# Eight unread loads of 1 to 8 partitions ahead of the first K tile of a cached-attention decode kernel

## The chip, the cores and the metric

The kernel runs on one core of one Trainium2 chip. The core has a matrix engine (TensorE, PE in the profile, with PEld for its weight loads), a vector engine (VectorE, DVE), a scalar engine (ScalarE, ACT), GpSimd (POOL) and SyncE (SP), which here does nothing but issue loads. Loads and stores are carried out by 16 DMA engines between HBM and the on-chip memory SBUF, which has 128 partitions. Time is the device time of one execution in microseconds, the median of the runs. A profiled execution gives the trace from which the views below are taken; its span is a little shorter than the time of the run.

## What is computed

One decode step for one token x of 448 numbers: grouped-query attention over a cache of 65536 positions (16 query heads, 8 key/value heads of 256), a gated feed-forward layer, and a sigmoid gate g that mixes the two.

```python
q = (x @ wq) -> 16 heads of 256
scores = q . k_cache * 256 ** -0.5        # each k/v head serves 2 query heads
a = (softmax(scores) . v_cache) @ wo
gate, up = x @ W_gate, x @ W_up
b = ((gate * (gate > 0)) * up) @ W_down
out = g * a + (1 - g) * b                 # g = sigmoid(sum(x * gate_w))
```

Everything is bfloat16. K and V caches are 8 x 65536 x 256 each, 537 MB together; the weights wq, wo, W_gate, W_up and W_down add some 12 MB. So nearly all of the work is to bring the caches in once.

## The kernel before

**Tiles and slots.** A tile is 128 partitions x 128 positions x 256, 64 KB in each partition, 8 MB in all; a head has four K tiles and four V tiles, which makes 32 and 32. Three ring buffers of that size (`ring[0..2]`, line 135) hold them. `order` (lines 206 to 220) writes the sequence of the loads by hand: wq, gate and up, K tile 0, W_down, K tiles 1, 2 and 3, and from then on one V tile (of the head before) after each K tile from tile 3 on. Near the end come pieces of wo and the last V tile in four pieces. Slots are given out in turn (line 236), and `freed` keeps for each load what must be finished before its slot is overwritten.

**Planner.** Each operation is given to an engine with a key, a planned time; `finish` sorts the operations of each engine by key, and that is the order of its program. Loads go to SyncE. `emit` puts a wait ahead of an operation for what it depends on. A load's semaphore counts 16 when it has landed. Loads of one queue are therefore issued in the order of their keys, and a load that waits for its slot holds up those behind it.

**The first loads.** The keys are 3.0 for the first 384 rows of wq (line 470, into `ring[2]`), 3.001 and 3.002 for gate and up (line 487), 3.01 for the tail of wq (line 471, into the first 2048 columns of `ring[1]`), 3.012 for the tail of gate (line 489). K tile 0 (line 535, into `ring[0]`) follows, then the tail of W_up in eight loads of four partitions (`rows64`, line 380), then W_down (line 522, into `ring[2]` once the q matmuls are done), then K tile 1 into `ring[1]`. `held` (line 230) names the first users of the slots: `ring[1]` is free for K tile 1 after `q`, the last q matmuls (line 327); `ring[2]` is free for K tile 2 after `gu` and `dn`, the feed-forward matmuls (lines 498 to 527).

**A K tile's way.** When it has landed, VectorE transposes it in two halves (line 353), TensorE forms the scores (lines 368 and 394; many matmuls of several functions are recorded under 394), VectorE and ScalarE take the maximum and the exponential (lines 541 to 545). The scores of a K tile free its slot. After the fourth K tile of a head its weights are rescaled and transposed (lines 551 to 571). A V tile needs only the matmuls of lines 441 and 394. The end is the wo matmuls (line 618), the copy out (line 623) and the store (line 625).

**Feed-forward.** Gate and up are multiplied early (line 498), their tails when they land (lines 506 and 510); VectorE applies gate and product (lines 516 to 520) between the two transposes of K tile 0, and TensorE the down projection (line 527).

Of the kernel before, what the change touches and what calls it, by code (L numbers as in the profile page):

```python
# [24 lines left out]
class _Plan:  # L25
# [13 lines left out]
    def dma(self, eng, key, sem, fn, deps=()):  # L39
        if sem not in self.dsem:  # L40
            self.dsem[sem] = self.es.enter_context(self.nc.semaphore("d_" + sem))
        o = _Op(eng, key, fn, deps, dma=sem)
        self.ops.append(o)
        return o
# [46 lines left out]
def bass_gated_mix__gqa_block_cached__glu_gated_reglu__decode_kernel(  # L91
# [39 lines left out]
    with es:  # L131
# [3 lines left out]
        ring = [sb("ring%d" % i, [128, U * DH], BF) for i in range(NRING)]  # L135
# [60 lines left out]
        op, dma = pl.op, pl.dma  # L196
# [30 lines left out]
        T_END = t + 20.0  # L227


        slot, held, freed = {}, {1: ["q"], 2: ["gu", "dn"]}, {}  # L230
        r = 0
        for kind, i, _ in order:
            if kind in ("k", "v") or (kind, i) in (("wo", 0), ("vp", 0)):
# [150 lines left out]
        l_, qk, smax, aexp, pv, last = {}, {}, {}, {}, {}, {}  # L384
# [83 lines left out]
        for kind, i, t in issue:  # L468
            if kind == "wq":
                l_["wq"] = dma("sp", t, "wq", lambda e: e.dma_start(wq3, A_wq[0:NR3, :].rearrange("(p k) n -> p (k n)", k=R3)))  # L470
                l_["wqh"] = dma("sp", t + 0.01, "wqh", lambda e: e.dma_start(
                    wqa, A_wq[NR3:D, :].rearrange("r (c n) -> (r c) n", c=2)))
                tq = tL["wq", 0]
# [57 lines left out]
            elif kind == "k":  # L531
                n = i
# [44 lines left out]
            elif kind in ("v", "vp"):  # L577
                if kind == "v":
                    n, lo, hi = i, 0, U
# [84 lines left out]
```

## Time and profile before

| | us |
|---|---|
| time, median of 2 runs | 1279.15 (1278.81 to 1279.49) |
| time of the profiled execution | 1278.8 |
| its span | 1277.3 |
| mean granted TensorE clock | 0.628 of full speed |

The busy times of the page are sums over the span. Its section on DMA counts packets: one packet is one contiguous piece that a DMA engine moved. In the list of issues a row names destination and source, the queue that issued (SPq is SyncE's), the number of loads of that kind, KB of each, and the median time from issue to landing in us. In the order in time, a row has start and duration in us, engine, line, operation, destination and source, a count, and in brackets the idle time of the engine before it and what ended it. In the table of stretches, a row has the stretch in us, its length, the busy time and instruction count of PE, PEld, DVE, ACT and POOL, then the granted clock, the busy share of the DMA engines and GB/s. A row of the waits has who waited for whom, the total in us, how often, and the longest.

### The profile page before, as it was taken

Reading aid. Unit: us, or ns where it says so; the run is one execution under the profiler, and the core shown is the slowest. Engines: PE = TensorE matmul, PEld = TensorE weight load, DVE = VectorE, ACT = ScalarE, POOL = GpSimd, SP = SyncE. Lnnn points to the kernel's source line nnn. Section 1 sums busy time; section 2 is a strip of 40 time slices with the busy share of each in tenths; the row PEclk is TensorE's granted clock in tenths of the full one; section 3 lists DMA queues with packets and bytes.
Section 4 is the critical chain, followed back from the end, with each engine's and each line's share of the span. In section 5 each row is a group of like instructions: output and inputs, shape, how many; then the busy total and the mean of one; then the engine's idle time right before and its main releaser. Section 6 shows DMA issues by size and latency. Waiting matters only on the chain.

```text
span 1277.3 us, 6839 instructions
## 1 busy us (share of the span) xinstructions
PE 353.3 (28%) x4410; PEld 71.3 (6%) x1862; DVE 688.2 (54%) x310; ACT 51.3 (4%) x84; POOL 7.3 (1%) x21
## 2 busy tenths in 40 slices
PE   3223223313122241133220242211332213223135
PEld 2000000000000000000000000000000000000001
DVE  3698743575534655445555554556535666336511
ACT  0000000000000000000000000000000000000000
POOL 2000000000000000000000000000000000000000
PEclk9566666665666575666755666656666556666576
DMA  9999999999999999999999999999999999999998
GB/s 405 442 426 431 438 437 432 427 433 438 435 429 427 439 434 433 434 429 433 432 435 436 431 432 429 436 441 429 427 434 437 436 429 427 438 439 432 427 428 352
DMA packets 11906, 549.46 MB, mean 430 GB/s; under 512 B 1315, under 2 KB 1574, under 8 KB 2790
## 3 DMA queue, kind: packets, MB, share of 16 engines
q1 hardware_dynamic: 11874, 549.03, 99.6%
q8 instruction: 24, 0.39, 0.1%
q14 instruction: 4, 0.03, 0.0%
q10 hardware_dynamic: 4, 0.00, 0.0%
HBM read 549.03 MB, written 0.00 MB: 430 GB/s over the span
## 4 chain that ended last, share of the span: by engine, by line
DVE 38%; DMA 31%; PE 17%; another core or an unknown queue 12%; issue 1%; SPq 0%; ACT 0%
DVE ring L353 31%; DMA ring<-in_A_k_cache_dram 28%; PE ST L368 5%; PE ST L394 5%; PE O L394 4%; DMA ring<-in_A_wo_dram 3%; DVE o_sb L403 2%; PE O L441 1%; DVE P L564 1%; DVE P L562 1%; DVE ST L541 1%; DVE nmb L543 1%; PE M_ps L569 0%; PE M_ps L557 0%
## 5 line engine op out<-in xcount | busy, mean ns | idle before, releaser
L353 DVE STREAM_TRANSPOSE ring<-ring 128x8192 uint32<-128x8192 uint32 x64 | 554.2, 8692 | 315.0 <-DMA ring<-in_A_k_cache_dram 315.0
L368 PE MATMUL ST<-ring,xm 128*16 128x512 bf16 x1024 | 141.6, 544 | 770.2 <-DVE ring L353 770.2
L394 PE MATMUL ST<-ring,xm 128*16 128x512 bf16 x1024 | 138.5, 532 | 0.0
L394 PE MATMUL O<-ring,P 128*32 128x512 bf16 x1512 | 117.2, 421 | 0.0
L541 DVE COPY_PREDICATED ST<-bm,ST 128x512 f32<-128x512 uint16 x32 | 22.2, 693 | 170.7 <-PE ST L394 170.7
L545 ACT ACTIVATE P<-ST,nmb 128x512 bf16<-128x512 f32 x32 | 45.4, 1417 | 1142.8 <-DVE nmb L543 1142.8
L368 PEld LDWEIGHTS ST<-ring,xm 128*16 128x16 bf16 x1024 | 32.2, 116 | 928.4 <-DVE ring L353 798.2
L441 PE MATMUL O<-ring,P 128*32 128x512 bf16 (+1 forms) x536 | 58.7, 438 | 27.3 <-DMA ring<-in_A_v_cache_dram 27.3
L403 DVE CAST_PREDICATED o_sb<-bm,O 128x512 bf16<-128x512 uint16 (+1 forms) x33 | 22.3, 679 | 62.6 <-PE O L394 56.4
L562 DVE TENSOR_TENSOR P<-P,hs 128x2048 bf16<-128x2048 bf16 x8 | 18.3, 2292 | 8.6 <-ACT hs L559 8.6
L441 PEld LDWEIGHTS O<-ring,P 128*32 128x32 bf16 (+1 forms) x536 | 16.0, 113 | 123.8 <-issue 91.5
L543 DVE TENSOR_REDUCE nmb<-ST 128x1 f32<-128x512 f32 x32 | 22.1, 691 | 1.1
L564 DVE STREAM_TRANSPOSE P<-P 128x2048 bf16<-128x2048 bf16 x8 | 18.5, 2311 | 0.3
L569 PE MATMUL M_ps<-hs,ones_f 128*128 128x2 f32 x16 | 4.7, 363 | 46.0 <-DVE hs L568 46.0
L421 PE MATMUL M_ps<-emat,o_sb 128*128 128x2 bf16 x72 | 3.3, 168 | 22.4 <-DVE o_sb L413 22.4
L545 ACT ACTIVATION_READ_ACCUMULATOR P<-ST,nmb 128x1 f32 x32 | 8.6, 268 | 0.0
L320 PE MATMUL M_ps<-ring,P 128*128 128x256 bf16 x48 | 7.6, 335 | 1.7 <-DMA ring<-in_A_wq_dram 1.7
L569 PEld LDWEIGHTS M_ps<-hs,ones_f 128*128 128x128 f32 x16 | 4.0, 311 | 46.7 <-DVE hs L568 46.7
L555 PE MATMUL M_ps<-identf,hs 128*2 128x128 f32 x8 | 2.2, 278 | 15.8 <-DVE hs L553 15.8
L320 PEld LDWEIGHTS M_ps<-ring,P 128*128 128x128 bf16 x48 | 5.6, 119 | 3.5 <-DMA ring<-in_A_wq_dram 1.8
L461 DVE TENSOR_SCALAR attnT<-M_ps,hs 64x4 bf16<-64x4 f32 x16 | 3.5, 221 | 3.8 <-PE M_ps L421 3.7
L618 PE MATMUL A_ps<-ring,attnT 128*1 128x224 bf16 x64 | 5.4, 320 | 0.2
(86 smaller groups left out, 70.5 us busy)
## 6 DMA issues: line engine op xcount, KB each, us to landing
ring<-in_A_v_cache_dram SPq DMA_DIRECT2D x1, 4096.0 KB, 29.8
ring<-in_A_wq_dram SPq DMA_DIRECT2D x1, 3072.0 KB, 10.3
ring<-in_A_v_cache_dram SPq DMA_DIRECT2D x1, 2048.0 KB, 34.3
ring<-in_A_v_cache_dram SPq DMA_DIRECT2D x2, 1024.0 KB, 37.3
ring<-in_A_wo_dram SPq DMA_DIRECT2D x4, 448.0 KB, 39.2
ring<-in_B_W_down_dram SPq DMA_DIRECT2D x1, 1568.0 KB, 23.4
ring<-in_B_W_gate_dram SPq DMA_DIRECT2D x1, 1344.0 KB, 13.0
ring<-in_B_W_up_dram SPq DMA_DIRECT2D x1, 1344.0 KB, 15.8
```

The lines of the kernel that those rows point to most:

```text
L320: ins = e.matmul(QN_ps, xw3[:, kt, 31 - j:159 - j], wq3[:, kt * NQ + j * 256:kt * NQ + (j + 1) * 256], start=(j == 0 and kt == 0), stop=Fa ...
L353: return lambda e: e.transpose(v, v)
L368: ins = e.matmul(o, xm[:, x0:x0 + 16], v, start=st, stop=False, skip_group_check=True, tile_position=(0, 32 * w))
L394: return e.add_instruction(mybir.InstMatmult(name=nc.get_next_instruction_name(), engine=e.engine, ins=[e.lower_ap(v), e.lower_ap(w, for_m ...
L403: return e.copy_predicated(dst, m.to_broadcast(list(src.shape)), src)
L441: ins = e.matmul(o, w, v, start=st, stop=False, skip_group_check=True, tile_position=(0, 32 * g))
L541: join = op("dv", tk + 25.2, lambda e: e.copy_predicated(ST[0][:], bm[:, NB:NB + 1].bitcast(mybir.dt.uint16).to_broadcast([128, 512]), ST[ ...
L543: smax[n] = op("dv", tk + 26, lambda e, n=n, NM=NM, t_=t_: e.tensor_reduce(NM[:, t_:t_ + 1], ST[0][:], AX.X, ALU.max, negate=True), [join, ...
L545: aexp[n] = op("ac", tk + 27, lambda e, n=n, t_=t_, NM=NM, RS=RS, Ph=Ph: e.activation(Ph[:, t_:2048:4], ST[0][:], ACTF.Exp, bias=NM[:, t_: ...
L562: rsc = op("dv", T + 16, lambda e, X=X, pb=pb: e.tensor_tensor(pb, pb, X[:, 12:16].unsqueeze(1).to_broadcast([128, 512, 4]), ALU.mult), [h ...
L564: last["ev", h] = [op("dv", T + 17, lambda e, Ph=Ph: e.transpose(Ph[:], Ph[:]), [rsc])]
L569: l3 = mop("pe", T + 19, lambda e, X=X: e.matmul(LS_ps, ones_f[:, :], X[:, 6:8], start=True, stop=True), [l2, c_one])
```

## The change

Eight loads are added to SyncE's queue. Load i, for i from 0 to 7, brings the first 3 x (i + 1) rows of wq, three rows of 8 KB for each partition, into i + 1 partitions of `ring[1]`: partition i // 2 and every eighth one after it, 24 KB in each, at column 8192 for even i and 20480 for odd i. No two loads write the same place, none touches the wq tail in the first 2048 columns, and nothing reads them. They share one semaphore, and K tile 1, which overwrites `ring[1]`, waits for it. Their keys, 3.02 to 3.027, put them after the tail of gate and before K tile 0. The result of the kernel does not depend on them.

```diff
-        slot, held, freed = {}, {1: ["q"], 2: ["gu", "dn"]}, {}
+        slot, held, freed = {}, {1: ["q", "pk"], 2: ["gu", "dn"]}, {}
...
             if kind == "wq":
                 l_["wq"] = dma("sp", t, "wq", lambda e: e.dma_start(wq3, A_wq[0:NR3, :].rearrange("(p k) n -> p (k n)", k=R3)))
+                for i in range(8):
+                    c = 8192 + i % 2 * 12288
+                    l_["pk"] = dma("sp", 3.02 + 0.001 * i, "pk", lambda e, i=i, c=c: e.dma_start(
+                        ring[1][i // 2:i // 2 + 8 * i + 1:8, c:c + 12288], A_wq[0:3 * i + 3, :].rearrange("(p k) n -> p (k n)", k=3)))
                 l_["wqh"] = dma("sp", t + 0.01, "wqh", lambda e: e.dma_start(
                     wqa, A_wq[NR3:D, :].rearrange("r (c n) -> (r c) n", c=2)))
```

## The prediction

> **What bounds the kernel now.** I read the busy times and slices of the page first, then the stretches, then the issues of the DMA queue, then the order in time of SyncE and of VectorE's big transposes.
>
> ```profile
> span 1277.3 us, 6839 instructions
> ...
> PE 353.3 (28%) x4410; PEld 71.3 (6%) x1862; DVE 688.2 (54%) x310; ACT 51.3 (4%) x84; POOL 7.3 (1%) x21
> ...
> DMA  9999999999999999999999999999999999999998
> ...
> DMA packets 11906, 549.46 MB, mean 430 GB/s; under 512 B 1315, under 2 KB 1574, under 8 KB 2790
> ...
> q1 hardware_dynamic: 11874, 549.03, 99.6%
> q8 instruction: 24, 0.39, 0.1%
> ...
> DVE 38%; DMA 31%; PE 17%; another core or an unknown queue 12%; issue 1%; SPq 0%; ACT 0%
> ```
>
> No compute engine is busy for more than 54% of the span, while SyncE's queue (q1) keeps the 16 DMA engines at work for 99.6% of it. The chain of waits gives DVE 38%, which misleads if read alone: it follows one tile's latency back, not the resource that is full. The stretches show at what rate that full resource runs:
>
> ```profile
> 0.00:20.00 20.00, 9.61 (x68) 7.44 (x69) 7.95 (x29) 1.49 (x2) 7.26 (x21) 1.00 0.94 385
> ...
> 80.00:1180.00 1100.00, 297.14 (x3795) 52.23 (x1491) 611.47 (x236) 45.82 (x74) 0.00 (x0) 0.62 1.00 433
> 1180.00:1200.00 20.00, 0.37 (x8) 0.29 (x8) 12.00 (x5) 0.00 (x0) 0.00 (x0) 0.50 1.03 446
> ...
> 1220.00:1225.00 5.00, 4.68 (x54) 1.00 (x18) 0.95 (x4) 0.00 (x0) 0.00 (x0) 0.62 0.78 330
> ```
>
> The last two columns are DMA share and GB/s: 433 GB/s at a share of 1.00 through the steady part, that is 433 / 16 = 27.06 GB/s for one engine. So the time is bytes over rate, and what counts is the bytes of the engine that has most of them: a tile has landed only when its last engine has brought its rows.
>
> **The queue must stay full for this to hold.** The issues, with the time from issue to landing:
>
> ```profile
> ring<-in_A_wq_dram SPq DMA_DIRECT2D x1, 3072.0 KB, 10.3
> ...
> ring<-in_B_W_down_dram SPq DMA_DIRECT2D x1, 1568.0 KB, 23.4
> ring<-in_B_W_gate_dram SPq DMA_DIRECT2D x1, 1344.0 KB, 13.0
> ring<-in_B_W_up_dram SPq DMA_DIRECT2D x1, 1344.0 KB, 15.8
> ...
> ring<-in_A_wq_dram SPq DMA_DIRECT2D x1, 512.0 KB, 16.6
> ring<-in_A_k_cache_dram SPq DMA_DIRECT2D x32, 50.4
> ring<-in_A_v_cache_dram SPq DMA_DIRECT2D x31, 34.8
> ...
> ring<-in_B_W_gate_dram SPq DMA_DIRECT2D x1, 224.0 KB, 16.6
> ring<-in_B_W_up_dram SPq DMA_DIRECT2D x8, 28.0 KB
> ```
>
> and the landings of K tiles, read from the start of the transpose that waited for each:
>
> ```profile
> 38.71 8.71 DVE L353 STREAM_TRANSPOSE ring<-ring 128x8192 uint32<-128x8192 uint32 x1 [15.19 <-DMA ring<-in_A_k_cache_dram]
> ...
> 63.55 8.71 DVE L353 STREAM_TRANSPOSE ring<-ring 128x8192 uint32<-128x8192 uint32 x1 [4.17 <-DMA ring<-in_A_k_cache_dram]
> ...
> 102.78 8.71 DVE L353 STREAM_TRANSPOSE ring<-ring 128x8192 uint32<-128x8192 uint32 x1 [0.70 <-DMA ring<-in_A_k_cache_dram]
> ...
> 141.48 17.30 DVE L353 STREAM_TRANSPOSE ring<-ring 128x8192 uint32<-128x8192 uint32 x2 [4.99 <-DMA ring<-in_A_k_cache_dram]
> ...
> 1188.48 17.30 DVE L353 STREAM_TRANSPOSE ring<-ring 128x8192 uint32<-128x8192 uint32 x2 [7.52 <-DMA ring<-in_A_k_cache_dram]
> ```
>
> From K tile 3 on a V tile lies between two K tiles, so 141.48 - 102.78 = 38.70 us is two tiles: 19.35 us each. A V tile lands 34.8 us after its issue, so 34.8 - 19.35 = 15.4 us of older work is still ahead of it. That is the reserve against a dry queue.
>
> **What a load of few rows does to the engines.** The added loads have 1 to 8 rows, so the first question is on how many engines such a load runs. Counted in the code, 80 loads have 128 rows (32 K, 31 V, 4 V pieces, 2 wq, 2 gate, 1 up, 1 down, 7 wo), the eight 28 KB loads of W_up have 4 partitions, and x, gate_w and out have one. If each load leaves one tiny packet on each engine that it uses, 80 x 16 + 8 x 4 + 3 = 1315, which is the page's count under 512 B to the unit. With the 4-row loads on 16 engines it would be 1411. So a 4-row load runs on 4 engines. Are they the same four each time? Between the landings of K tiles 0 and 1 lie 63.55 - 38.71 = 24.84 us; one tile is 19.35, W_down (1.606 MB at 433 GB/s) 3.71, which leaves 1.78 us for the eight 28 KB loads. On the same four engines they cost 229,376 B / (4 x 27.06 GB/s) = 2.12 us, spread over all 16 only 0.53. The 1.78 is near the 2.12 (the engine last with tile 0 need not be one of the four). Small loads pile up on the same engines. The same 1.78 us speaks for no fixed cost by the load. [...]
>
> **The bytes, step by step.** Load i (0 to 7) has i + 1 rows of 24 KB, together 36 rows, 864 KB. If they pile up as W_up's do, each load starting at the same engine, that engine gets 8 rows, the next 7, and so on to the eighth with 1; the other eight get none. One row: 24,576 B / 27.06 GB/s = 0.908 us. First engine: 8 x 0.908 = 7.3 us. Since that engine never runs dry and all K and V tiles give it the same eighth-of-128 share as the others, the delay stays with it to the end, and the last landing moves by as much.
>
> Two corrections. The price of a row may be higher at the start of the program: the wq load has the same packets, eight rows of 24 KB on each engine, and took 10.3 us from issue to landing, first latency and receipt included. So the eight rows cost 7.3 to 10.3. And part may be hidden: from K tile 3 to K tile 31 are 28 x 2 = 56 tiles, 1083.6 us at 19.35, but 1188.48 - 102.78 = 1085.70, so the latest engine has fallen back by 2.1 us during the run (the 24 instruction packets on q8 are the likely cause, 0.1% of 16 x 1277.3 us). If those are other engines than the first, 2.1 us of lateness exist already and the added lateness goes beside them. So 5.2 to 10.3 in all. The corrections have opposite signs and about the same size, so I take the plain row at steady rate, 7.3.
>
> **Issue and waits.** SyncE's start:
>
> ```profile
> 2.75 0.51 SPq L489 DMA_DIRECT2D ring<-in_B_W_gate_dram  x1
> 3.30 0.45 SPq L535 DMA_DIRECT2D ring<-in_A_k_cache_dram  x1
> 3.82 5.47 SPq L380 DMA_DIRECT2D ring<-in_B_W_up_dram  x8
> 20.80 0.35 SPq L522 DMA_DIRECT2D ring<-in_B_W_down_dram  x1
> 21.19 44.11 SPq L535 DMA_DIRECT2D ring<-in_A_k_cache_dram  x3
> ```
>
> Eight more issues at 0.45 (the K row) to 0.68 us (5.47 / 8) are 3.6 to 5.5 us of SyncE. K tile 0 then goes out at 6.9 to 8.8 instead of 3.30. Ahead of it on the engines lie 3072 + 1344 + 1344 + 512 + 224 = 6496 KB, 6.65 MB, at 385 GB/s 17.3 us of work, so the issue costs nothing; it would cost its excess if it came after 17. The W_up pieces go out by 14.8 instead of 9.3, still before W_down, which waits until 20.80 for the q matmuls (wq and its tail are ahead of the new loads and do not move). K tile 1 gains a wait: its slot now also needs the new loads landed, at 17.3 + 7.3 = 24.6 to 28 us by queue order, instead of issue at 21.19. Queued behind it on SyncE are K tiles 2 and 3. Tile 0 lands only at 38.71, so the cover is 10 us or more: price zero. K tile 2 is the longest one to look at:
>
> ```profile
> SPq L535 <- PE A_ps L527: 32.0, 1, 32.0
> ```
>
> It waits 32.0 us for the down projection, which follows tile 0's first transpose on VectorE and so moves with tile 0's landing, 21.5 + 32.0 = 53.5 to about 60.8. On the late engine tile 1 then ends at 63.55 + 7.3 = 70.9, 10 us later; the early engines may idle for a microsecond, which they have to spare. Later the reserve of 15.4 us shrinks to 8 us on the engines that are not late, and stays whole on the late one. Near the end, at 1220 to 1225, the share falls to 0.78: there the early engines wait for the last full V tile, the late ones set the landing.
>
> Sum: the profiled run took 1278.8 us for a span of 1277.3; 1278.8 + 7.3 = 1286.1. It lies 0.35 under the median of the two runs, so by the median 1279.15 + 7.3 = 1286.4, slower by 0.6%.
>
> **Rivals.**
> *Even spread, or loads that cost no more than their bytes:* 884,736 B at 433 GB/s is 2.0 us, 1281.2. For it: the mean rate is what the page reports. Against it: the count of 1315. The case that the loads are not done, or that an idle stretch near the end swallows the lateness, gives 1279 to 1281. Together 0.09.
>
> *Two engines in turn at one door of SBUF:* in the loads of five to eight rows, the rows lie on partitions 8 apart, so the first and the fifth are 32 apart. If two engines that write partitions 32 apart are served in turn, four of the first engine's rows cost double: 12 x 0.908 = 10.9 us, less 0 to 2.1 hidden, 1288.0 to 1290.1. For it: the steady rate is read from loads of all 128 partitions, so it cannot exclude that single rows placed otherwise get in each other's way. Against it: no stretch of the trace shows engines slowing each other. I give it 0.28. [...]
>
> *Another rate:* staggered engines might meet less often at HBM. The best stretch shows 446 GB/s; all of 1100 us at that is 1100 x (1 - 433/446) = 32 us less, 1279 - 32 + 7 = 1254, faster by 1.9%. Against it: the share there is 1.03, so 446 / 1.03 is the same 433; the packets were booked differently, not faster. 0.02.
>
> *The reserve is used up (slower by over 2%):* if the lateness grew past 15.4 us, a V tile would be issued to an empty queue on most engines, and if this also delayed the late one, each of the 31 rounds would lose the excess; 0.9 us a round is 28 us, 1314 with the 7.3. It decides from a lateness of 15.4; the upper end of my price is 10.9. 0.02.
>
> **Numbers.** The forecast has 0.59, with 5.2 to 8.2 us, 1284.3 to 1287.4; the port case 0.28. Together 0.87, from 1284.3 to 1290.1; with half a microsecond for the noise of two runs and a hidden part that may be somewhat over 2.1, the range is 1283 to 1290.5. Measured against 2%, about what a measurement of this kernel can tell from no change (1253.6 and 1304.7), all of these are within; faster has 0.01, slower 0.02.
>
> **What would show it.** Packets under 512 B: 1315 + 36 = 1351, if every load uses as many engines as rows. K tile 0 transposed from about 46.0 and tile 1 from 70.9, against 40.7 and 65.6 with an even spread and 49.6 and 74.4 in the port case. K tile 31 shows what was hidden: 1195.8 if nothing, 1193.7 if 2.1. GB/s unchanged at 433 in the steady part; anything else would make the whole sum wrong.

## The result, and the profile after

The changed kernel takes 1288.58 us, median of 2 runs (1288.44 to 1288.72), against 1279.15 before: 9.4 us more, ratio 1.0075 with a 95% interval of 1.0058 to 1.0092. It is slower, clear of noise, by less than 2%. Lines behind the new loads are 4 higher in the new code (K tiles: 539 in place of 535); the new loads are recorded at line 473.

First the page of the changed kernel: span, busy times, packets, SyncE's queue, the chain of waits.

```profile
span 1287.2 us, 6847 instructions
...
PE 349.1 (27%) x4410; PEld 70.1 (5%) x1862; DVE 688.3 (53%) x310; ACT 51.2 (4%) x84; POOL 7.1 (1%) x21
...
DMA packets 11978, 550.35 MB, mean 428 GB/s; under 512 B 1351, under 2 KB 1610, under 8 KB 2826
...
q1 hardware_dynamic: 11946, 549.92, 99.4%
...
DVE 38%; DMA 31%; PE 17%; another core or an unknown queue 12%; issue 1%; SPq 1%; ACT 0%
```

Compute is as before, and the chain's shares too, so they do not tell the two kernels apart. What did change is counted: 72 packets more, 36 of them under 512 B (1315 to 1351), 0.89 MB more. Where the time went is seen in the landings of the K tiles, read as before from the start of the transposes that waited for them. The rows are tile 0, tile 1 and tile 31 of the changed kernel:

```profile
50.25 8.71 DVE L353 STREAM_TRANSPOSE ring<-ring 128x8192 uint32<-128x8192 uint32 x1 [26.70 <-DMA ring<-in_A_k_cache_dram]
...
75.59 8.71 DVE L353 STREAM_TRANSPOSE ring<-ring 128x8192 uint32<-128x8192 uint32 x1 [4.67 <-DMA ring<-in_A_k_cache_dram]
...
1197.96 17.30 DVE L353 STREAM_TRANSPOSE ring<-ring 128x8192 uint32<-128x8192 uint32 x2 [7.97 <-DMA ring<-in_A_k_cache_dram]
```

Tile 0 starts 11.5 us later than before (38.71), tile 1 12.04 us later (63.55), tile 31 only 9.48 us later (1188.48). So the whole loss is there before the second K tile, and 2.56 us of it are gone by the last. The stretches (the last two columns are DMA share and GB/s) show the place. The changed kernel:

```profile
20.00:25.00 5.00, 2.31 (x33) 0.83 (x18) 2.23 (x11) 0.37 (x1) 0.00 (x0) 1.00 1.03 231
25.00:30.00 5.00, 0.00 (x0) 0.00 (x0) 0.00 (x0) 0.00 (x0) 0.00 (x0) 0.74 0.79 297
...
80.00:1180.00 1100.00, 287.75 (x3699) 50.79 (x1463) 619.15 (x232) 45.74 (x74) 0.00 (x0) 0.62 1.00 433
```

and the kernel before in the first two of these:

```profile
20.00:25.00 5.00, 2.28 (x33) 0.80 (x18) 2.23 (x11) 0.37 (x1) 0.00 (x0) 1.00 0.97 419
25.00:30.00 5.00, 0.00 (x0) 0.00 (x0) 0.00 (x0) 0.00 (x0) 0.00 (x0) 0.57 1.03 446
```

In the steady part nothing changed: 433 GB/s. But while the added loads pass, the 16 engines together fall to 231 GB/s, with all of them busy by the record (share 1.03).

The trace also holds one record for each packet, with its queue, size, start and duration, but without the engine's number. These records are read here and in the experiments below beside the views. Of the 36 packets of 24 KB that the added loads bring, 32 took 1.2 to 1.9 us, against 0.91 for a packet of that size in the running wq load. The 64 KB packets of K tile 0 that started at 18 to 20 us took 4.4 to 5.0 us, against 2.42 before. Counted as they overlap 25 to 30 us, the packets keep all engines busy there too; the share of 0.79 in the view comes from packets that were booked in the stretch before. So packets took twice as long, and no engine was without work. At 18 to 20 us eight of these 64 KB packets run beside eight of the added rows, so engines that were not bringing an added row at that time were slowed as well. The prediction's forecast had no such dip; its port rival (two engines in turn at one door) had it for a few engines.

SyncE's issues and waits after (start, duration, line; then who waited for what, total, times, longest):

```profile
3.33 5.49 SPq L473 DMA_DIRECT2D ring<-in_A_wq_dram  x8
8.86 0.45 SPq L539 DMA_DIRECT2D ring<-in_A_k_cache_dram  x1
...
20.83 0.33 SPq L526 DMA_DIRECT2D ring<-in_B_W_down_dram  x1
30.86 46.20 SPq L539 DMA_DIRECT2D ring<-in_A_k_cache_dram  x3
```

```profile
SPq L539 <- PE A_ps L531: 34.0, 1, 34.0
...
SPq L539 <- DMA ring<-in_A_wq_dram: 9.7, 1, 9.7
```

K tile 1 waits 9.7 us for the added loads and goes out at 30.86, 19 us before tile 0 is transposed: the queue does not run dry on it.

### The profile page after: what moved, and what is told of

It reads as the page before. It is cut to its first block, busy times and chain, and to the rows that moved or that the text cites. A ratio compares the mean times of both kernels' runs of the same rounds, so it can differ in the third digit from the quotient of the medians.

```text
span 1287.2 us, 6847 instructions
## 1 busy us (share of the span) xinstructions
PE 349.1 (27%) x4410; PEld 70.1 (5%) x1862; DVE 688.3 (53%) x310; ACT 51.2 (4%) x84; POOL 7.1 (1%) x21
## 2 busy tenths in 40 slices
DMA packets 11978, 550.35 MB, mean 428 GB/s; under 512 B 1351, under 2 KB 1610, under 8 KB 2826
## 4 chain that ended last, share of the span: by engine, by line
DVE 38%; DMA 31%; PE 17%; another core or an unknown queue 12%; issue 1%; SPq 1%; ACT 0%
DVE ring L353 30%; DMA ring<-in_A_k_cache_dram 28%; PE ST L368 5%; PE ST L394 5%; PE O L394 4%; DMA ring<-in_A_wo_dram 3%; DVE o_sb L403 2%; PE O L441 1%; DVE P L568 1%; DVE P L566 1%; DVE ST L545 1%; DVE nmb L547 1%; SPq L473 0%; PE M_ps L573 0%
```

## The experiments

Three questions were open. Why does a row of 24 KB cost more than its bytes? Where do 2.6 us go between tile 1 and tile 31? And is it the engines' load that counts, or the place in the queue and the new wait? Each kernel below is the changed one but for the lines shown, timed against the kernel before on the same chip. "Tile 1" and "tile 31" are the starts of their transposes, less those of the kernel before.

The expectations speak of doors of SBUF, and of rows that share one. That is the author's assumption: no run shows a door or which partitions would share it; the runs show what each placement costs.

| | tile 1 | tile 31 | time, us | ratio to before (95%) |
|---|---|---|---|---|
| the change | +12.04 | +9.48 | 1288.58 | 1.0075 (1.0058 to 1.0092) |
| step 4 | +7.06 | +4.48 | 1283.35 | 1.0034 (1.0021 to 1.0047) |
| other source | +11.84 | +9.27 | 1288.42 | 1.0074 (1.0057 to 1.0091) |
| even | +1.90 | +2.35 | 1280.99 | 1.0016 (1.0007 to 1.0026) |
| one row, eight loads | +7.07 | +4.47 | 1283.48 | 1.0036 (1.0023 to 1.0049) |
| one row, four loads | +3.83 | +1.24 | 1279.89 | 1.0007 (0.9998 to 1.0016) |
| one row, two loads | +1.57 | -0.19 | 1279.09 | 1.0001 (0.9992 to 1.0010) |
| step 1 | +17.74 | +15.18 | 1293.39 | 1.0110 (1.0094 to 1.0127) |
| upper half, step 4 | +14.83 | +12.35 | 1291.10 | 1.0095 (1.0080 to 1.0110) |
| pair 32 apart | +14.46 | +12.01 | 1291.14 | 1.0096 (1.0079 to 1.0113) |
| four rows, step 8 | +14.89 | +14.03 | 1293.05 | 1.0111 (1.0094 to 1.0128) |
| four rows, step 4 | +7.42 | +6.23 | 1285.01 | 1.0047 (1.0032 to 1.0062) |
| W_up tail in two loads (no added loads) | +1.27 | +2.16 | 1281.20 | 1.0019 (1.0010 to 1.0029) |

### Other partitions, same bytes

```diff
-                        ring[1][i // 2:i // 2 + 8 * i + 1:8, c:c + 12288], A_wq[0:3 * i + 3, :].rearrange("(p k) n -> p (k n)", k=3)))
+                        ring[1][i // 2:i // 2 + 4 * i + 1:4, c:c + 12288], A_wq[0:3 * i + 3, :].rearrange("(p k) n -> p (k n)", k=3)))
```

> The eight loads as in the change, but row k of a load goes to partition i // 2 + 4 k instead of i // 2 + 8 k; same bytes, same sources, same engines. Theory A (engines that write partitions sharing one door of SBUF hold each other up, and all others with them): with step 4 no two engines share a door, so a row costs 0.91 us, the first engine is 7.3 us late, K tile 0 is transposed from 45.2 to 46.0 us instead of 50.25, GB/s stays near 430 between 20 and 25 us, and the time is 1283.5 to 1285.5. Theory B (several engines reading the same few rows of wq crowd one place in HBM) and theory C (loads of few rows cost 1.4 us a row whatever their addresses): as the change, K tile 0 at 50, time 1288 to 1289.

Tile 1 and the stretch from 20 to 25 us with step 4:

```profile
70.61 8.71 DVE L353 STREAM_TRANSPOSE ring<-ring 128x8192 uint32<-128x8192 uint32 x1 [4.75 <-DMA ring<-in_A_k_cache_dram]
```

```profile
20.00:25.00 5.00, 2.30 (x33) 0.82 (x18) 2.23 (x11) 0.37 (x1) 0.00 (x0) 1.00 1.03 446
```

The dip is gone (446 against 231 GB/s), the first engine's eight rows cost 7.06 us at tile 1, close to the 7.3 of bytes over rate, and the time is 1283.35, a hair under the lower end expected. Only the destinations differ, so 5 of the 12 us are a matter of where the rows land. By the packet records each of the 36 rows took 0.91 to 0.93 us.

### Other source, same partitions

```diff
-                        ring[1][i // 2:i // 2 + 8 * i + 1:8, c:c + 12288], A_wq[0:3 * i + 3, :].rearrange("(p k) n -> p (k n)", k=3)))
+                        ring[1][i // 2:i // 2 + 8 * i + 1:8, c:c + 12288], A_k_cache[0, i, 0:48 * i + 48, :].rearrange("(p u) d -> p (u d)", u=48)))
```

> The eight loads as in the change, destinations with step 8 too, but each load reads its own stretch of the K cache (load i from head i) instead of the first rows of wq. Theory A: nothing changes, K tile 0 from about 50.2 us, time 1288 to 1289, GB/s near 231 between 20 and 25 us. Theory B: the crowding is gone, K tile 0 from 45.2 to 46.0, time 1283.5 to 1285.5. Theory C: as A.

```profile
75.39 8.71 DVE L353 STREAM_TRANSPOSE ring<-ring 128x8192 uint32<-128x8192 uint32 x1 [4.68 <-DMA ring<-in_A_k_cache_dram]
```

```profile
20.00:25.00 5.00, 2.56 (x35) 1.05 (x21) 2.23 (x11) 0.37 (x1) 0.00 (x0) 1.00 0.92 208
```

Nothing is gained by reading elsewhere: 208 GB/s and 1288.42. Theory B falls; with step 4, theory C has fallen too.

### The same bytes on all engines

```diff
-                for i in range(8):
-                    c = 8192 + i % 2 * 12288
-                    l_["pk"] = dma("sp", 3.02 + 0.001 * i, "pk", lambda e, i=i, c=c: e.dma_start(
-                        ring[1][i // 2:i // 2 + 8 * i + 1:8, c:c + 12288], A_wq[0:3 * i + 3, :].rearrange("(p k) n -> p (k n)", k=3)))
+                l_["pk"] = dma("sp", 3.02, "pk", lambda e: e.dma_start(
+                    ring[1][:, 8192:8192 + 3456], A_wq[0:128, 0:3456]))
```

> The same 864 KB in one load of 128 partitions, 6.75 KB each, at the same place in the queue. If the cost of the change is that the bytes are unevenly laid on the engines (A, B and C alike), all 16 engines are 2.0 us late, K tile 0 is transposed from 40.7, and the time is 1281 to 1281.5. If the cost were in the place in the queue or in the wait of K tile 1 for the loads, it would stay at 1288 to 1289.

Measured: 1280.99, 2.0 us over the before of the same chip (1279.01), against 884,736 B at 433 GB/s = 2.04. Place in the queue and bytes are the same. So of the change's 9.4 us the bytes as such are 2.0, the place nothing that can be seen, and the rest is how they are laid on the engines and the partitions.

This kernel says little of the wait, though: its loads land early, and K tile 1 waits 0.3 us for them instead of 9.7. That the wait costs nothing is shown by a kernel further below, the pair: there K tile 1 goes out at 33.31, later than the 30.86 of the change, and its lateness is no more than what 16 rows in turn take.

### One engine alone

```diff
-                        ring[1][i // 2:i // 2 + 8 * i + 1:8, c:c + 12288], A_wq[0:3 * i + 3, :].rearrange("(p k) n -> p (k n)", k=3)))
+                        ring[1][i // 2:i // 2 + 1, c:c + 12288], A_wq[0:3, :].rearrange("(p k) n -> p (k n)", k=3)))
```

> Eight loads of one row of 24 KB each, to partitions 0 to 3: 192 KB in all, every row on the first engine by the theory of piling up. Theory A: that engine has its door to itself, 8 x 0.91 = 7.3 us late, K tile 0 from 45.2 to 46.0, no dip of GB/s for the others, time 1283.5 to 1285.5 after what is hidden. Theory C: 8 x 1.4 = 11 us, K tile 0 from 49 to 50, time 1287 to 1289. If a single row were cut over the 16 engines instead: 0.5 us, time 1279.5.

The packets and tile 1 of this kernel:

```profile
DMA packets 11922, 549.66 MB, mean 429 GB/s; under 512 B 1323, under 2 KB 1582, under 8 KB 2798
```

```profile
70.62 8.71 DVE L353 STREAM_TRANSPOSE ring<-ring 128x8192 uint32<-128x8192 uint32 x1 [4.70 <-DMA ring<-in_A_k_cache_dram]
```

Eight tiny packets more (1315 to 1323): one engine for each load. 192 KB delay tile 1 as much as the 864 KB of the step-4 kernel (+7.07 and +7.06). The latest engine alone sets the landing; the other 28 rows of step 4 are free. This also shows that the eight loads start at the same engine. The packet records agree. A load ends on each engine with a packet of 4 bytes; for tile 1 fifteen of the sixteen end between 60.5 and 63.0 us, as they do before, and one at 70.1.

### What is hidden at the end

The one-row kernel with four loads, and with two:

```diff
-                for i in range(8):
+                for i in range(4):
```

```diff
-                for i in range(8):
+                for i in range(2):
```

> As the one-row experiment, but four loads instead of eight: 3.65 us on the first engine. Theory H (part is hidden because by the end other engines are late by themselves; what shows at the end is the lateness at K tile 1 less a fixed 2.6 us, and not below zero): K tile 1 from 67.0, K tile 31 0.8 us later than before, at 1189.3, time 1279.8. If a fixed share of the lateness is lost (4.5 of 7.1 us, 0.63): K tile 31 at 1190.6, time 1281.2. If nothing is lost: 1282.5.

> Two one-row loads: 1.8 us on the first engine. Theory H: K tile 1 from 65.1, K tile 31 as before, 1188.4 to 1188.6, time 1279.0. Fixed share: K tile 31 at 1189.5, time 1280.0. Nothing lost: 1280.5.

Tiles 1 and 31 with two loads:

```profile
65.12 8.71 DVE L353 STREAM_TRANSPOSE ring<-ring 128x8192 uint32<-128x8192 uint32 x1 [4.70 <-DMA ring<-in_A_k_cache_dram]
...
1188.29 17.30 DVE L353 STREAM_TRANSPOSE ring<-ring 128x8192 uint32<-128x8192 uint32 x2 [8.57 <-DMA ring<-in_A_k_cache_dram]
```

With two loads, tile 1 is 1.57 us late and tile 31 not at all; the time is that of before. With four, 3.83 and 1.24, each 0.4 us over what was expected. The difference is 2.59, as with eight (2.60), with step 4 (2.58) and in the change (2.56): a fixed amount, not a share (four loads would have left 2.4 us by the share of 0.63). So theory H holds. It is also visible in one kernel. From tile 1 to tile 31 lie 58 tiles, 1122.3 us at 19.35; the change takes 1197.96 - 75.59 = 1122.37, its latest engine loses nothing on the way. Before, 1188.48 - 63.55 = 1124.93: there another engine falls behind and is the latest by the end.

The packet records of the kernel before show why. An instruction packet (q8, 16 KB) takes 1.0 to 1.1 us, and as soon as it ends a 64 KB packet starts that takes 2.9 to 3.0 us instead of 2.42; so one fetch costs its engine about 1.5 us. Between tile 1 and tile 31 lie 21 of them, 21 x 1.5 = 32 us. The sixteen engines together fall behind by 35 us on that way, by their last packets of the two tiles against 58 tiles of 19.35 us. Instruction fetches are thus nearly all of what makes other engines late; no kernel without them was run.

### Neighbouring partitions, and the upper half

Two kernels press the same point harder: rows on neighbouring partitions, and step 4 from partition 64 up.

```diff
-                        ring[1][i // 2:i // 2 + 8 * i + 1:8, c:c + 12288], A_wq[0:3 * i + 3, :].rearrange("(p k) n -> p (k n)", k=3)))
+                        ring[1][i // 2 * 16:i // 2 * 16 + i + 1, c:c + 12288], A_wq[0:3 * i + 3, :].rearrange("(p k) n -> p (k n)", k=3)))
```

```diff
-                        ring[1][i // 2:i // 2 + 8 * i + 1:8, c:c + 12288], A_wq[0:3 * i + 3, :].rearrange("(p k) n -> p (k n)", k=3)))
+                        ring[1][64 + i // 2:64 + i // 2 + 4 * i + 1:4, c:c + 12288], A_wq[0:3 * i + 3, :].rearrange("(p k) n -> p (k n)", k=3)))
```

> The eight loads with their rows on neighbouring partitions (step 1 instead of 8; load i starts at partition 16 x (i // 2)). Theory A: four engines now write each of two doors, one of which takes the 26 rows of the first four engines in turn; worked out by equal shares, the first engine's rows end 16.4 to 17.2 us after the start of the loads instead of 12, K tile 1 is transposed from 79.7 to 80.5 us (before 63.55), and after 2.6 us hidden the time is 1292.5 to 1293.5. If only engines that write partitions exactly 32 apart hold each other up, no two do here: K tile 1 from 70.6, 1283.4.

> [...] Theory A: each row takes turns with a K packet, 16 x 0.91 = 14.5 us on the first engine, K tile 1 from about 77.8, time 1290 to 1291 after 2.6 hidden. If only the added loads hold each other up: as step 4, K tile 1 from 70.6, time 1283.4.

Tile 1 with step 1, and in the upper half:

```profile
81.29 8.71 DVE L353 STREAM_TRANSPOSE ring<-ring 128x8192 uint32<-128x8192 uint32 x1 [4.67 <-DMA ring<-in_A_k_cache_dram]
```

```profile
78.38 8.71 DVE L353 STREAM_TRANSPOSE ring<-ring 128x8192 uint32<-128x8192 uint32 x1 [4.66 <-DMA ring<-in_A_k_cache_dram]
```

Step 1 gave 1293.39, as expected, with tile 1 at 81.29, 0.8 us beyond the expected end. The upper half gave 1291.10 and tile 1 at 78.38, 0.1 and 0.6 us over. Both far from the 1283.4 of loads that stay out of each other's way. Step 1 and the upper half have the same bytes in the same loads as step 4 (7.06 us), yet cost 17.74 and 14.83, and from 20 to 25 us the engines together bring 203 and 213 GB/s, against 446. In neither do two rows of one load lie 32 apart, so the destination's share of the price is not confined to such loads.

### Whom a clash holds up

The pair, then four rows with step 8 and with step 4, each in place of the same line:

```diff
-                        ring[1][i // 2:i // 2 + 8 * i + 1:8, c:c + 12288], A_wq[0:3 * i + 3, :].rearrange("(p k) n -> p (k n)", k=3)))
+                        ring[1][i // 2:i // 2 + 33:32, c:c + 12288], A_wq[0:6, :].rearrange("(p k) n -> p (k n)", k=3)))
```

```diff
+                        ring[1][i // 2:i // 2 + 25:8, c:c + 12288], A_wq[0:12, :].rearrange("(p k) n -> p (k n)", k=3)))
```

```diff
+                        ring[1][i // 2:i // 2 + 13:4, c:c + 12288], A_wq[0:12, :].rearrange("(p k) n -> p (k n)", k=3)))
```

> Eight loads of two rows, on partitions 32 apart (i // 2 and i // 2 + 32), so that the first and the second engine write through one door and nothing else is shared: 384 KB. Theory A: the 16 rows pass in turn, 14.5 us, K tile 1 transposed from 77.6 to 78.5 us, time 1290 to 1291. It also tells whom the door holds up. If only the two engines that use it: the other fourteen keep their rate and GB/s between 20 and 25 us is 433 - 27 = 406. If every engine with work in flight is held up behind it: near the 231 of the change. Without any shared door (theories B, C) two rows a load would give 70.6 and 1283.4.

> Eight loads of four rows with step 8: 768 KB on the first four engines, 7.3 us each. [...] Theory A: 14.5 us on the third and the fourth engine, K tile 1 transposed from 77.3 to 78.5, time 1290 to 1291.5. [...] If only partitions exactly 32 apart clash: as step 4, 1283.4.

> [...] Theory H with four late engines instead of one, of which the latest counts: K tile 31 from 1193.0 to 1194.9, time 1283.4 to 1285.3.

Tile 1 and the stretch from 20 to 25 us; the pair:

```profile
78.01 8.71 DVE L353 STREAM_TRANSPOSE ring<-ring 128x8192 uint32<-128x8192 uint32 x1 [4.66 <-DMA ring<-in_A_k_cache_dram]
```

```profile
20.00:25.00 5.00, 2.36 (x33) 0.88 (x19) 2.23 (x11) 0.37 (x1) 0.00 (x0) 1.00 0.98 396
```

four rows with step 8:

```profile
78.44 8.71 DVE L353 STREAM_TRANSPOSE ring<-ring 128x8192 uint32<-128x8192 uint32 x1 [4.70 <-DMA ring<-in_A_k_cache_dram]
```

```profile
20.00:25.00 5.00, 2.32 (x33) 0.85 (x18) 2.23 (x11) 0.37 (x1) 0.00 (x0) 1.00 1.00 206
25.00:30.00 5.00, 0.00 (x0) 0.00 (x0) 0.00 (x0) 0.00 (x0) 0.00 (x0) 0.55 0.99 206
```

four rows with step 4:

```profile
70.97 8.71 DVE L353 STREAM_TRANSPOSE ring<-ring 128x8192 uint32<-128x8192 uint32 x1 [4.71 <-DMA ring<-in_A_k_cache_dram]
...
1194.71 17.30 DVE L353 STREAM_TRANSPOSE ring<-ring 128x8192 uint32<-128x8192 uint32 x2 [8.15 <-DMA ring<-in_A_k_cache_dram]
```

The pair is the clean case: two engines, eight rows each, partitions 32 apart, and tile 1 is 14.46 us late: 16 rows in turn, 14.5. The time, 1291.14, is 0.1 us over the expected range. The other fourteen keep their rate (396, near the 406 expected). By the packet records the added rows took 1.81 us each from the third on, twice 0.91, while nearly every 64 KB packet beside them kept its 2.42 to 2.46 us. Four rows show the effect of the step alone: 7.42 us with step 4 (418 GB/s from 20 to 25 us), 14.89 with step 8. But theory A in its simple form, that only the engines that take turns lose, fails here. If two engines' rate were lost, 433 - 2 x 27 = 379 GB/s would be left, an estimate from the steady rate; 206 were measured, half rate for everything that was in flight, and the time of 1293.05 lies 1.5 us over the expected range. The packet records agree: with step 8 all 64 KB packets that started from 20 to 28 us took 5.0 to 5.1 us, and the twelve engines that carry no added row ended tile 1 at 68.0 to 69.8 us, against 60.4 to 62.1 with step 4. Some placements hold up all engines, the pair does not. No experiment here separates why; in the pair two engines take turns, and whether the number of engines that do so decides was not tested.

Four late engines instead of one hide less at the end (7.42 to 6.23, 1.2 us instead of 2.6). By the packet records the four end tile 1 between 70.0 and 70.6 us, and the last of them loses 1.0 us between 590 and 650 us, where at 618 us an instruction packet of another queue (q14, 8 KB) is followed by a 64 KB packet of 3.08 us. The lone late engine of the one-row kernel has no such loss.

### A load that is there already

The kernel before, without added loads; the tail of W_up in two loads of 16 partitions instead of eight of 4.

```diff
-            Wr = W[NR3:D, :].rearrange("(b g a c) f -> g c a b f", b=2, g=2, a=4, c=4)
-            for i in range(8):
-                g, c = divmod(i, 4)
-                d_ = dma("sp", t + 0.0001 * i, sem, lambda e, g=g, c=c: e.dma_start(
-                    wfu[32 * g + c:32 * g + c + 13:4, :, :], Wr[g, c]), deps)
+            Wr = W[NR3:D, :].rearrange("(b g q) f -> g q b f", b=2, g=2, q=16)
+            for g in range(2):
+                d_ = dma("sp", t + 0.0001 * g, sem, lambda e, g=g: e.dma_start(
+                    wfu[32 * g:32 * g + 16, :, :], Wr[g]), deps)
```

> The kernel before, without the eight added loads; the tail of W_up comes in two loads of 16 neighbouring partitions instead of eight loads of 4 partitions four apart. The bytes then lie on all 16 engines, 14 KB each, instead of 56 KB on each of four. If only an engine's bytes count: 0.5 us on every engine, K tile 1 about 1.5 us earlier than before, at 62.0, and the end within 0.5 us of before, 1279.0 to 1279.6. Theory A: the 32 rows still pass through four doors, four engines at each, 2.1 us, and now all 16 engines are in them: K tile 1 at 63.3 to 63.9, K tile 31 2 us later at 1190.5, time 1281.

Tiles 1 and 31:

```profile
64.82 8.71 DVE L353 STREAM_TRANSPOSE ring<-ring 128x8192 uint32<-128x8192 uint32 x1 [4.03 <-DMA ring<-in_A_k_cache_dram]
...
1190.64 17.30 DVE L353 STREAM_TRANSPOSE ring<-ring 128x8192 uint32<-128x8192 uint32 x2 [7.64 <-DMA ring<-in_A_k_cache_dram]
```

Measured 1281.20, 2.4 us over before (1278.77 on the same chip). Fewer loads of more rows are slower. That speaks against an engine's bytes alone, by which tile 1 was to start at 62.0 and the time to be 1279.0 to 1279.6. It agrees with theory A at the end (1190.5 and 1281 expected, 1190.64 and 1281.20 measured), by which all 16 engines are late, the ones that are latest at the end among them; that the rows pass through four doors no run shows. The packet records show that all are late: the sixteen engines end tile 1 at 62.5 to 64.4 us, where before eleven of them end it at 60.4 to 61.3 and five at 62.3 to 63.1. Tile 1 came 0.9 us later than that theory gave, so some hold-up comes on top. No experiment beat the kernel before.

## Why the prediction was right, step by step

The range held, by luck in part. The forecast's own band, 1284.3 to 1287.4, was missed by 1.2 us, and its mechanism, rows at the steady rate on one engine, accounts for 7.06 of the 12.04 us at tile 1. The measured time lies in the range because the range reached over the port rival.

**The bound** held: time is the bytes of the latest engine over its rate. The steady part has 433 GB/s in both kernels; 7.06 against 7.07 us for 864 KB and 192 KB shows that only the latest engine counts. (The "eighth-of-128 share" of the prediction is eight rows of 128, a sixteenth.)

**Piling up** held: 1351 packets under 512 B as said, and one-row loads that all delay the same engine (7.07 us for eight). The count of packets under 512 B fits as many engines as rows for the added loads of one to eight rows (36 more in the change, 8 more with one-row loads); which of the 16 engines these are no run shows.

**The price of a row** was the term that was mis-sized: "the eight rows cost 7.3 to 10.3", of which 7.3 was taken. With step 4 it is 7.06, so bytes over rate was sound for rows that stay out of other engines' way. On the partitions of the change it is 12.04, beyond both bounds. The upper bound came from the wq load, which has the same packets; by the packet records the first row on each engine took 1.3 to 2.1 us there and every later one 0.91 to 0.94, so its 10.3 us hold a start that the added rows did not have, and its 128 rows could not show what a few rows elsewhere cost.

**The hidden part**, "0 to 2.1", was 2.56 from tile 1 to tile 31. The mechanism is shown by the two- and four-load kernels, and the cause that the prediction called likely, the instruction packets, is borne out by the packet records. The size was counted from tile 3 on, too late by half a microsecond.

**The net**, 7.3, was to be right because two corrections cancel. They did not: +4.7 and -2.6 (12.04 - 7.3; 2.56).

**The port rival**, two engines in turn at one door, given 0.28 against 0.59, is what happened: 1288.0 to 1290.1 was its time, and tiles 0 and 1 were to start at 49.6 and 74.4, measured 50.25 and 75.59. It had 10.9 us at tile 1 and up to 2.1 hidden, against 12.04 and 2.56, two misses that partly cancel. The pair shows the turns: 16 x 24,576 B in 14.46 us are 27.2 GB/s for two engines with rows 32 apart, the rate of one (27.06 in the steady part). No run shows that the third and the fourth engine of the four rows with step 8, or the rows of the upper half, take turns with packets of K tile 0, as the 14.5 us of their expectations suppose; in their place the runs showed 14.89 us at 206 GB/s and 14.83 us at 213 GB/s. The rival was right in kind, incomplete in extent: the change also slows engines that bring no added row at the time (eight 64 KB packets of 4.4 to 5.0 us against 2.42), 231 GB/s in all.

**Issue and waits** held, at nothing: K tile 0 issued at 8.86 (said: 6.9 to 8.8), K tile 1 at 30.86 (24.6 to 28, later because the loads landed later), K tile 2 after 34.0 us for the down projection (32.0 before). The even load, at the same place, costs its bytes only; the pair, with a longer wait, costs its rows only.

**Even spread** as an alternative gave 2.0 us, and the even load measured 2.0. **Another rate** and **the used-up reserve** did not occur: 433 GB/s, and 2.6 us regained between tile 1 and tile 31, none lost.

## What to carry to other kernels

In a kernel that keeps all DMA engines busy, cost a load of few rows by the engine that gets most rows, not by its bytes: 192 KB on one engine cost as much as 864 KB (7.07 and 7.06 us). Then look at where the rows land: by their partitions alone the same bytes took up to 2.5 times as long (17.74 against 7.06 us at tile 1), and in all the slow placements but the pair the other engines were slowed too (203 to 231 GB/s from 20 to 25 us; the pair 396). A lateness stays to the end unless other engines are late by then (2.6 us of it here); the check is the landing of an early and of a late tile, not the total.

## What was not expected of the hardware

A placement of four rows, 768 KB in all, held the traffic of all 16 engines at half rate, 206 GB/s from 20 to 30 us, while the pair, with 16 rows in turn, left 396. What the pair lacks stays open.

The issue cost on SyncE went with where the rows lie: the eight loads take 5.49 us with step 8 and with step 4 alike (5.50 in the upper half), and with step 1, on neighbouring partitions, for the same rows:

```profile
3.29 2.70 SPq L473 DMA_DIRECT2D ring<-in_A_wq_dram  x8
```

It lies beside the queue's work in both.
